# The opening of a two-layer transformer kernel: two head groups' queries first, the other queries and values after the first scores

## The chip, the cores and the metric

The kernel runs on one core of a Trainium2 chip. A core has five engines with instruction queues of their own: TensorE (PE, matrix products; its weight loads are listed as PEld), VectorE (DVE), ScalarE (ACT), GpSimd (POOL) and SyncE (SP, which here issues all DMAs). Each queue is worked off in its order, and queues wait for each other by semaphores. The metric is the device time of one execution in microseconds (us), as the median of several runs.

## The reference, cut to what matters

The input is 2048 tokens of 512 numbers in bf16. Attention and a feed-forward part follow each other twice, with the same weights in both rounds; each works on a layer norm and adds to its input.

```python
def _A_ref(x, wqkv, wo):
    B, S, D = x.shape
    H = 32; Dh = D // H
    qkv = (x @ wqkv).reshape(B, S, 3, H, Dh).transpose(2, 0, 3, 1, 4)
    q, k, v = qkv[0], qkv[1], qkv[2]
    p = _softmax(jnp.einsum("bhqd,bhkd->bhqk", q, k) * Dh ** -0.5, axis=-1)
    o = jnp.einsum("bhqk,bhkd->bhqd", p, v)
    return o.transpose(0, 2, 1, 3).reshape(B, S, D) @ wo

def _B_ref(x, w1, b1, w2, b2):
    y = _layernorm(x, axis=-1)
    h = _gelu(jnp.einsum("bsd,df->bsf", y, w1) + b1)
    return jnp.einsum("bsf,fd->bsd", h, w2) + b2

x = A_x
x = x + _A_ref(_layernorm(x, axis=-1), A_wqkv, A_wo)
x = x + _B_ref(_layernorm(x, axis=-1), B_w1, B_b1, B_w2, B_b2)
x = x + _A_ref(_layernorm(x, axis=-1), A_wqkv, A_wo)
x = x + _B_ref(_layernorm(x, axis=-1), B_w1, B_b1, B_w2, B_b2)
```

There are 32 heads of 16 numbers; four heads form a head group, so there are eight head groups. The work that counts is 32 x 2048 x 2048 exponentials in each of the two attention parts.

## The kernel before, in words

**How the order of the work comes about.** The program is a generator. Jobs (`job_lnqkv`, `job_first_tile`, `flow_scores` and others) are Python coroutines that hand tasks to a planner, `Sched`. A task names its engine, a priority (smaller goes first), its instructions, what they read and write, and for each a written-down duration. The planner plays time forward with these durations: at each step it takes, on the engine that can start first, the ready task of the smallest priority, and appends it to that engine's queue. A changed duration, priority or task can thus change the order of everything after it. Buffers and PSUM banks are handed out by pools (`get` and `release`), and a job can wait for marks set by others (`keys`). A second pass, `refill`, puts products with a zero matrix (`zw`, lines L1307 to L1311) into planned gaps of PE, to keep its clock up.

**Attention.** Tokens are cut into 16 tiles of 128, queries into chunks of 512 (four tiles). A segment is one head group and one chunk of queries over some key tiles; a score tile is one key tile against 512 queries of one head. The first chunk is run in two parts: part 0 takes only the key tiles 0 to 3 for all eight head groups (16 score tiles for each), so that scores can begin when four token tiles have been worked up; part 1 takes the other twelve. `flow_scores` sends score tiles in groups, two tiles alternating between two pairs of banks in part 0, and three and two tiles from part 1 on. ACT takes the exponential of a group (L1386). From part 1 on VectorE takes a share of the tiles with an integer trick (L1478, L1509). PE multiplies the exponentials by the values (L1579). A group of scores needs the scaled queries of its segment (`qt`) and the key and value of its key tile (`kv`).

**The softmax bound.** Each query row carries, as a 17th number in a 32-wide slot, an upper bound of its scores taken from the query's norm and the largest key norm, so that no maximum over scores is needed. For this the keys' squares are summed (`norms`, L992, into `n2k`), the maximum over tokens is taken, its square root formed on POOL (L1109), and two small matmuls spread it (`job_scl`, L1104 to L1113). The queries' side is `bound_rows` (L999 to L1007): an inverse square root by an integer start value and one Newton step, in six small operations.

**The opening.** Three loads of x and three of the weights go out first (`build_startup`). Six buffers for query and key rows (`qk`) have their padding cleared (L724, L725, L758, L759). For each of the first four token tiles `ln_group` makes the norm's statistics on VectorE (L850, L851) and the inverse root on POOL (L858, L859), and `job_first_tile` does the rest: it applies the norm (L870), transposes on PE (L1020) and copies on ACT (L1021), and starts three strands. `keys` multiplies (L1043), copies to bf16 (L1054), squares on ACT (L1057), sums, and stores a transposed copy into KT by DMA (L1047). `queries` multiplies for all 32 heads, copies and squares on ACT (L1066, L1067), sums, forms the bound, transposes the first head group's queries on PE (L1072) and stores all of them to memory (`q_scr`, L1075). `values` multiplies and copies on ACT (L1082). `job_qt` multiplies the queries by the scale (L1144): the first head group straight from PSUM, the others from a transposed load of `q_scr` (L1130). When the queries of all four tiles are on their way to memory (mark `qst`), the tiles 4 to 15 begin: statistics, norm on POOL (L868), a transposing DMA (L904), keys and values (`job_qkv_tile`, L927 to L950), and last their queries. When the keys of all 16 tiles are known, `job_scl` runs again for part 1.

Of the kernel before, what the change touches and what calls it, by code (L numbers as in the profile page):

```python
# [8 lines left out]
BF16 = mybir.dt.bfloat16  # L9
F16 = mybir.dt.float16  # L10
F32 = mybir.dt.float32
I32 = mybir.dt.int32
# [499 lines left out]
class Builder:  # L512
# [45 lines left out]
    def alloc(self, es):  # L558
# [51 lines left out]
        self.qt2 = t("qt2", [128, 4, 32], F32)  # L610
        self.kmx = t("kmx", [32, 4], F32)
# [5 lines left out]
        self.nmr = t("nmr", [128, 16], F32)  # L617
        self.ioi = self.dp[:, 6, 0:256].bitcast(F32)
# [17 lines left out]
        pl["qk"] = Pool(range(3))  # L636
# [49 lines left out]
    def build_startup(self):  # L686
# [28 lines left out]
        dve = lambda fn, reads, writes, dur=0.2: Task("dve", 1.9, [I(fn, reads, writes, dur)])  # L715
# [6 lines left out]
        def pads(eng, b):  # L722
            qv = self.qks(b)
            n0(eng, I(lambda e: e.memset(qv.rearrange("p k (h c) -> p (k h) c", c=32)[:, :, 16:32], 0.0), [], [("qk", b, 0), ("qk", b, 1)], 0.9))  # L724
            n0(eng, I(lambda e: e.memset(qv[:, 1, :].rearrange("p (h c) -> p h c", c=32)[:, :, 16:17], 1.0), [], [("qk", b, 0), ("qk", b, 1)], 0.2))  # L725
# [3 lines left out]
        pads("pool", 0)  # L729
        pads("pool", 1)  # L730
        pads("dve", 2)

        def consts():
            vv = self.V[:, :, :, :, :].rearrange("p g k h d -> p (g k h) d")
            yield dve(lambda e: e.memset(vv[:, :, 16:17], 1.0), [], [("V", hg, kb) for hg in range(8) for kb in range(16)], 0.7)
# [14 lines left out]
    def build_startup_late(self):  # L750
# [4 lines left out]
        def fills():  # L755
            for b in range(3, 6):
                qv = self.qks(b)
                yield Task("pool", 4.0, [I(lambda e, qv=qv: e.memset(qv.rearrange("p k (h c) -> p (k h) c", c=32)[:, :, 16:32], 0.0), [], [("qk", b, 0), ("qk", b, 1)], 0.9),  # L758
                                         I(lambda e, qv=qv: e.memset(qv[:, 1, :].rearrange("p (h c) -> p h c", c=32)[:, :, 16:17], 1.0), [], [("qk", b, 0), ("qk", b, 1)], 0.2)])  # L759
                S_.release("qk", b)  # L760
# [84 lines left out]
    def ln_group(self, tiles, slot, prio, eps1, eps0, shift):  # L845

        for i, tt in enumerate(tiles):
            c = 4 * slot + i
            s = yield ("get", "st")
            yield Task("dve", prio, [I(lambda e, s=s, tt=tt: e.bn_stats(out=self.st[:, s, :], in_=self.xres[:, tt, :]), [("x", tt)], [("st", s)], 0.65)])  # L850
            yield Task("dve", prio, [I(lambda e, s=s, c=c: e.bn_aggr(out=self.mv[:, c, :], in_=self.st[:, s, :]), [("st", s)], [("mv", c)], 0.172)])  # L851
            self.S_.release("st", s)
# [5 lines left out]
        yield Task("pool", prio, [I(lambda e: e.tensor_scalar(out=rs, in0=var, scalar1=eps1, scalar2=eps0, op0=ALU.mult, op1=ALU.add), [("mv", c0 + i) for i in range(n)], [R], 0.2)])  # L858
        yield Task("pool", prio, [I(lambda e: e.tensor_tensor(out=rs, in0=rs, in1=self.cneg[:, 0:n], op=ALU.pow), [R, ("cneg",)], [R], 0.45 + 0.15 * n)])  # L859
# [16 lines left out]
    def job_lnqkv(self, L, tiles, prio, later=None):  # L876
# [6 lines left out]
        for i, tt in enumerate(tiles):  # L883
            if L == 1 and tt < 4:
                self.S_.spawn(self.job_first_tile(tt, slot, i, left, prio), prio)
                continue
# [6 lines left out]
    def job_qkv_tile(self, L, tt, slot, i, left, prio, what):  # L893
# [4 lines left out]
        yield self.ln_apply(tt, slot, i, xnr, RX, prio, "dve" if tt >= 12 else "pool")  # L898
# [87 lines left out]
    def norms(self, dst, res, ss, which):  # L986
# [3 lines left out]
        def fn(e):  # L990
            with self.nc.allow_low_precision(reason="rounded once, in a bound with a margin"):
                return e.tensor_reduce(out=dst, in_=self.sqs(ss)[:, a:a + 32, :], axis=AX.X, op=ALU.add)  # L992
        return I(fn, [("sq", ss, which)], [res], 0.67)

    def bound_rows(self, qs, ns, RN, prio, eng="pool"):

        pads = lambda ap: ap.rearrange("p (h c) -> p h c", c=32)
        QQ = ("qk", qs, 0)
        yield Task("dve", prio, [I(lambda e: e.tensor_scalar(out=self.qy[:, ns, :], in0=self.n2[:, ns, :].bitcast(I32), scalar1=-0.5, scalar2=RSQRT_MAGIC, op0=ALU.mult, op1=ALU.add), RN, [("qy", ns)], 0.18)])  # L999
        y = self.qy[:, ns, :].bitcast(F32)  # L1000
        a, c, x = self.qt1[:, ns, :], self.qt2[:, ns, :], self.n2[:, ns, :]
        RA, RC = ("qt1", ns), ("qt2", ns)
        yield Task(eng, prio, [I(lambda e: e.tensor_tensor(out=a, in0=x, in1=y, op=ALU.mult), RN + [("qy", ns)], [RA], 0.25 if eng == "pool" else 0.2)])
        yield Task(eng, prio, [I(lambda e: e.tensor_tensor(out=c, in0=a, in1=y, op=ALU.mult), [RA, ("qy", ns)], [RC], 0.25 if eng == "pool" else 0.2)])
        yield Task(eng, prio, [I(lambda e: e.tensor_scalar(out=c, in0=c, scalar1=-0.5, scalar2=1.5, op0=ALU.mult, op1=ALU.add), [RC], [RC], 0.217 if eng == "pool" else 0.2)])
        yield Task(eng, prio, [I(lambda e: e.tensor_tensor(out=a, in0=a, in1=c, op=ALU.mult), [RA, RC], [RA], 0.25 if eng == "pool" else 0.2)])
        yield Task(eng, prio, [I(lambda e: e.tensor_scalar(out=pads(self.qks(qs)[:, 0, :])[:, :, 16:17], in0=a.rearrange("p (n o) -> p n o", o=1), scalar1=-MARG, scalar2=0.0, op0=ALU.mult, op1=ALU.add),  # L1007
# [931 lines left out]
```

## Time and profile before

The time is 1595.41 us, the median of three runs (1594.99 to 1596.77). The profiled execution has a span of 1594.1 us.

| what | from the profile |
|---|---|
| busy share of the span | PE 97%, ACT 96%, DVE 91%, POOL 21% |
| exponentials on ACT (L1386) | 1274 instructions, 1449.7 us |
| first exponential starts | 24.77 us |
| first group of three score tiles | 89.60 us |
| DVE busy in the first 24.77 us | 20.04 us |
| ACT busy in the first 24.77 us | 11.73 us |
| POOL busy in the first 24.77 us | 15.07 us |
| matmuls for queries, keys and values of tiles 0 to 3 (L1043) | 10.16 to 21.44 us |
| first matmul for tiles 4 to 15 (L927) | 35.86 us |
| second scale ready to be read (L1113 starts) | 84.56 us |

How to read the profile: a row of the timeline gives the start and the length in us, the engine, the line of the kernel, the operation, what it writes and reads, how many instructions are merged in the row, and in brackets how long the engine stood idle before it and what ended that. In the table of groups the two numbers behind the bar are busy time in us and the mean of one instruction in ns. The chain of waits is followed back from the end: at each step to what released it. A busy PE includes the zero products, and several row-tiled matmuls at once count once.

### The profile page before, as it was taken

To read this page: it belongs to the slowest core of one execution; us is meant where nothing else is said; L and a number is where in the kernel's file an instruction comes from. 1 tells how busy PE (TensorE), PEld (TensorE's weight loads), DVE (VectorE), ACT (ScalarE), POOL (GpSimd) and SP (SyncE) were. 2 spreads that over 40 slices of the span, in tenths; PEclk is the share of its full clock that TensorE was granted. 3 is DMA by queue.
4 is the path that set the end of the run, shared out by engine and by line. 5 is a ranking of instruction groups with operands and counts; after the bars stand their busy time and mean duration, and the time that the engine had idled before them with its cause. 6 is when DMAs were issued, how large, how long until landed. Compare 5 with 4: busy or idle time off the path is not lost.

```text
span 1594.1 us, 39159 instructions
## 1 busy us (share of the span) xinstructions
PE 1538.6 (97%) x16364; PEld 479.4 (30%) x16497; DVE 1450.3 (91%) x3202; ACT 1528.0 (96%) x1357; POOL 333.9 (21%) x574
## 2 busy tenths in 40 slices
PE   9999999999999999999999999999999999999998
PEld 3222222222222222222222223222222222344444
DVE  7689999989999899989999898999899989999793
ACT  6999999999999999989999998999999999999996
POOL 5585312001220012103212217310001000020010
PEclk9999999999999999999999999999999999999999
DMA  6662012112321223223722233211101100221100
GB/s 172 116 142 87 29 31 40 48 41 59 81 48 50 44 53 78 57 53 86 139 44 62 53 68 78 61 25 21 34 14 38 28 19 22 40 48 30 41 25 21
DMA packets 212465, 88.80 MB, mean 56 GB/s; under 512 B 183835, under 2 KB 206656, under 8 KB 212288
## 3 DMA queue, kind: packets, MB, share of 16 engines
q1 hardware_dynamic: 212288, 86.29, 24.0%
q8 instruction: 129, 2.11, 0.6%
q14 instruction: 48, 0.39, 0.1%
HBM read 34.65 MB, written 19.48 MB: 34 GB/s over the span
## 4 chain that ended last, share of the span: by engine, by line
PE 51%; DVE 28%; ACT 17%; issue 2%; POOL 0%; DMA 0%; POOLq 0%; DVEq 0%
PE ps L1401 18%; ACT PT L1386 15%; PE ps L1579 15%; DVE dp L1478 12%; DVE dp L1509 9%; PE ps L1713 4%; PE ps L1756 4%; PE ps L927 3%; PE ps L1307 3%; ACT h L1748 1%; PE ps L1311 1%; PE ps L1658 1%; DVE accT L1609 1%; DVE st L850 1%; DVE n L992 1%
## 5 line engine op out<-in xcount | busy, mean ns | idle before, releaser
L1386 ACT ACTIVATE PT<-ps 128x1536 bf16<-128x1536 f32 (+1 forms) x1274 | 1449.7, 1259 | 38.8 <-PE ps L1401 32.2
L1401 PE MATMUL ps<-QT,KT 32*128 32x512 bf16 (+1 forms) x4608 | 672.3, 358 | 16.8 <-DVE dp L1478 5.5
L1478 DVE TENSOR_SCALAR dp<-ps 128x512 uint16<-128x512 f32 x944 | 632.6, 681 | 61.2 <-PE ps L1401 58.2
L1509 DVE TENSOR_SCALAR dp<-dp 128x1024 uint16<-128x1024 uint16 (+1 forms) x1434 | 557.4, 430 | 7.9 <-PE ps L1579 3.2
L1579 PE MATMUL ps<-PT,V 128*17 128x512 bf16 (+1 forms) x3544 | 467.1, 358 | 0.0
L1579 PE MATMUL ps<-dp,vs 128*17 128x512 bf16 (+1 forms) x3192 | 444.4, 357 | 0.5 <-DVE dp L1509 0.2
L1401 PEld LDWEIGHTS ps<-QT,KT 32*128 32x128 bf16 x4608 | 172.2, 91 | 546.4 <-ACT PT L1386 237.3
L1144 POOL TENSOR_SCALAR QT<-qraw,scl,qbias 128x512 bf16<-128x512 bf16 (+1 forms) x84 | 72.2, 860 | 790.0 <-PE ps L1401 784.8
L1579 PE MATMUL ps<-dp,V 128*17 128x512 bf16 (+1 forms) x1064 | 215.3, 357 | 1.3 <-DVE accT L1609 1.0
L1309 PE MATMUL ps<-zw 32*128 32x444 bf16 (+5 forms) x702 | 193.5, 323 | 0.0
L1579 PEld LDWEIGHTS ps<-dp,vs 128*17 128x17 bf16 x3192 | 111.0, 88 | 130.3 <-issue 106.8
L1579 PEld LDWEIGHTS ps<-PT,V 128*17 128x17 bf16 x3544 | 113.2, 88 | 102.5 <-issue 89.6
L1311 PE MATMUL ps<-zw 128*32 128x448 bf16 (+22 forms) x1477 | 136.5, 323 | 0.4 <-DVE dp L1478 0.2
L1307 PE MATMUL ps<-zw 128*128 128x448 bf16 (+17 forms) x481 | 114.1, 333 | 4.0 <-DVE ps L727 1.7
L1713 PE MATMUL ps<-yT,wf 128*128 128x512 bf16 (+3 forms) x353 | 92.9, 356 | 8.6 <-issue 4.4
L927 PE MATMUL ps<-wqkv,xnT 128*128 128x512 bf16 x299 | 85.8, 382 | 7.6 <-issue 3.5
L1609 DVE STREAM_TRANSPOSE accT<-ps 128x512 f32<-128x512 f32 (+1 forms) x88 | 57.9, 658 | 10.8 <-PE ps L1579 9.9
L1737 DVE TENSOR_SCALAR h<-ps,b1c 128x512 bf16<-128x512 f32 (+2 forms) x88 | 62.3, 708 | 5.0 <-PE ps L1713 4.7
L1579 PEld LDWEIGHTS ps<-dp,V 128*17 128x17 bf16 x1064 | 53.1, 88 | 45.2 <-issue 27.3
L1169 POOL TENSOR_SCALAR vs<-V 128x340 bf16<-128x340 bf16 (+2 forms) x72 | 60.5, 842 | 26.3 <-PE ps L1579 21.2
L1307 PEld LDWEIGHTS ps<-zw 128*128 128x128 bf16 x481 | 37.4, 98 | 74.2 <-issue 46.4
L1311 PEld LDWEIGHTS ps<-zw 128*32 128x32 bf16 x1477 | 49.1, 95 | 22.1 <-DVE dp L1478 4.1
(179 smaller groups left out, 892.2 us busy)
## 6 DMA issues: line engine op xcount, KB each, us to landing
vs<-vs_scr SPq DMA_DIRECT2D x56, 255.0 KB, 2.8
wf<-in_B_w_dram SPq DMA_DIRECT2D x90, 128.0 KB, 2.6
q_scr<-qk SPq DMA_DIRECT2D x22, 256.0 KB, 2.1
k_scr<-qk SPq DMA_DIRECT2D x12, 256.0 KB, 2.0
out_dram<-xres SPq DMA_DIRECT2D x16, 128.0 KB, 1.7
vs_scr<-vs SPq DMA_DIRECT2D x8, 255.0 KB, 2.9
xres<-in_A_x_dram SPq DMA_DIRECT2D x7, 256.0 KB, 3.3
v_scr<-vst SPq DMA_DIRECT2D x12, 136.0 KB, 1.7
```

The lines of the kernel that those rows point to most:

```text
L927: yield Task("pe", prio, [I(lambda e, c=c: e.matmul(self.ps[:, b, :], lhsT=xnT[:, c, :], rhs=self.wqkv[:, c, which * 512:which * 512 + 512 ...
L1144: yield Task(eng, 0.4, [I(lambda e: e.tensor_scalar(out=self.QT[:, q, 0:W], in0=src, scalar1=self.scl[:, k, hg:hg + 1], scalar2=self.qbias ...
L1307: fn = lambda e: e.matmul(self.ps[:, b, 0:w], lhsT=self.zw[:, 0:128], rhs=self.zw[:, 0:w], start=st, stop=st, skip_group_check=True)
L1309: fn = lambda e: e.matmul(self.ps[:, b, 0:w], lhsT=self.zw[32 * p:32 * p + 32, 0:128], rhs=self.zw[32 * p:32 * p + 32, 0:w], start=st, sto ...
L1311: fn = lambda e: e.matmul(self.ps[32 * p:32 * p + 32, b, 0:w], lhsT=self.zw[:, 0:32], rhs=self.zw[:, 0:w], start=st, stop=st, skip_group_c ...
L1386: S_.submit(Task("act", 1e-5 * gi, [I(lambda e, pt=pt, n=n, b0=b0: e.activation(out=self.PT[:, pt:pt + n, :], in_=self.ps[:, b0:b0 + n, :] ...
L1401: return [I(lambda e, kb=kb, i=i: e.matmul(self.ps[:, b, i * W:(i + 1) * W], lhsT=self.KT[32 * hp:32 * hp + 32, hg, kb * 128:(kb + 1) * 12 ...
L1478: self.S_.submit(Task("dve", 0.0, [I(lambda e: e.tensor_scalar(out=self.dp[:, u, w * 512:(w + 1) * 512], in0=self.ps[:, b, :], scalar1=BIT ...
L1509: yield Task("dve", pr, [I(lambda e, k=k, v=v: e.tensor_scalar(out=self.dp[:, v, 0:N], in0=self.dp[:, u, 0:N], scalar1=float(SHIFT[k]), sc ...
L1579: ops.append((nth[j, sh] + 0.1 * i, I(lambda e, hp=hp, v=v, ap=ap[:, i * W:(i + 1) * W], first=first and i == 0, W=W: e.matmul(self.ps[32 ...
L1609: yield Task("dve", 0.3, [I(lambda e: e.transpose(self.accT[:, a, 0:W], self.ps[:, ACCB, 0:W]), [("ps", ACCB)], [RA], 0.17 + 0.535 * W / 5 ...
L1713: yield Task("pe", pr, [I(lambda e, c=c: e.matmul(self.ps[0:M, b, off:off + W], lhsT=self.w1(fc, c), rhs=self.yT[:, c, 0:W], start=(c == 0 ...
```

## The change

Its aim is to put less in front of the first scores. In words:

- Only the queries of the head groups 0 and 1 (128 of 512 columns) are made on the way to the first scores, for all four tiles into one bank (`job_q0`): one copy, one square, one sum and one bound on VectorE for all four tiles together, eight transposes into one bank, and both head groups scaled straight from PSUM.
- The queries of the other six head groups are multiplied after all keys, and their sums and bounds wait until the second head group's queries are scaled (`("qt", 1)`). The store to `q_scr` is in two pieces.
- The value of tile 0 waits for the other queries' matmuls, the values of tiles 1 to 3 for `("qt", 1)`; those of tiles 2 and 3 are copied by VectorE.
- GpSimd has fewer fills: two padding buffers go to ACT and two to VectorE, two and the ones of V remain on GpSimd, and the other fills wait for the fourth tile's key norms. The root's two steps are one task, and tiles 2 and 3 share one norm group. For tiles 4 to 7 the norm is applied by VectorE.
- The query scaling of the first segment of part 1 (index 8) moves from GpSimd to VectorE, and several priorities and written-down durations change.

```diff
         def pads(eng, b):
             qv = self.qks(b)
-            n0(eng, I(lambda e: e.memset(qv.rearrange("p k (h c) -> p (k h) c", c=32)[:, :, 16:32], 0.0), [], [("qk", b, 0), ("qk", b, 1)], 0.9))
...
+            hole = qv.rearrange("p k (h c) -> p (k h) c", c=32)[:, :, 16:32]
+            if eng == "pool":
+                n0("pool", I(lambda e: e.memset(hole, 0.0), [], [("qk", b, 0), ("qk", b, 1)], 0.95))
+            elif eng == "act":
+                n0("act", I(lambda e: e.activation(out=hole, in_=self.zw[:, 0:16].unsqueeze(1).broadcast_to([128, 64, 16]), func=ACTF.Copy), [("zw",)], [("qk", b, 0), ("qk", b, 1)], 1.05))
...
+            n0("dve" if eng == "act" else eng, I(lambda e: e.memset(qv[:, 1, :].rearrange("p (h c) -> p h c", c=32)[:, :, 16:17], 1.0), [], [("qk", b, 0), ("qk", b, 1)], 0.2))
...
-        pads("pool", 0)
-        pads("pool", 1)
-        pads("dve", 2)
+        self.P.free["act"] = 2.0
+        for b in (2, 3):
+            pads("act", b)
+        for b in (0, 1):
+            pads("dve", b)
...
+        for b in (4, 5):
+            pads("pool", b)
...
         def queries():
+            b = self.qfbank
+            yield from mm(0, 128, b, prio - 0.4, 128 * tt)
+            S_.mark(("q0mm", tt))
+            yield ("keys", [("kmm", k) for k in range(4)])
             b = yield ("get", "mb")
-            yield from mm(0, b, prio)
...
+            yield from mm(128, 512, b, prio + 0.4)
+            S_.mark(("qrm", tt))
...
+            yield ("keys", [("qt", 1)])
+            yield Task("dve", prio + 0.2, [self.norms(self.n2[:, ns, 8:32], ("n2", ns), ss, 0, 8)])
+            yield from self.bound_rows(qs, ns, [("n2", ns)], prio - 0.3, "pool", 8)
             done()
...
         def values():
+            yield ("keys", [("qrm", k) for k in range(4)] if tt < 1 else [("qt", 1)])
             b = yield ("get", "mb")
...
+    def job_q0(self):
...
+        S_.submit(Task("act", 0.4, [I(lambda e: e.activation(out=rows[:, :, 0:16], in_=src, func=ACTF.Copy, scale=0.25 * YU), [("ps", b)], Q0, 0.63)]), cb=lambda: S_.release("mb", b))
+        yield Task("act", 0.3, [I(lambda e: e.activation(out=self.q0sq, in_=src, func=ACTF.Square, scale=0.25 * YU), [("ps", b)], [("dp", 6, 1)], 0.63)])
+        yield Task("dve", 0.3, [I(lambda e: e.tensor_reduce(out=self.q0n[:, 0, :], in_=self.q0sq, axis=AX.X, op=ALU.add), [("dp", 6, 1)], [("n2", "q0")], 0.68)])
+        yield from self.bound(*[self.q0n[:, k, :] for k in range(4)], "q0", rows[:, :, 16:17], ("dp", 7, 0), [("n2", "q0")], 0.3, "dve")
...
-        eng = "dve" if sg["i"] < 4 else "pool"
+        eng = "dve" if sg["i"] in (0, 1, 2, 3, 8) else "pool"
...
-        for tt in range(4):
-            S_.spawn(self.job_lnqkv(1, [tt], 1.5 + 0.1 * tt), 1.5 + 0.1 * tt)
+        S_.spawn(self.job_q0(), 0.3)
+        for ts in ([0], [1], [2, 3]):
+            S_.spawn(self.job_lnqkv(1, ts, 1.5 + 0.1 * ts[0]), 1.5 + 0.1 * ts[0])
```

## The prediction

> **What bounds the kernel now.** First view, the page: the sums and the costliest group.
>
> ```profile
> PE 1538.6 (97%) x16364; PEld 479.4 (30%) x16497; DVE 1450.3 (91%) x3202; ACT 1528.0 (96%) x1357; POOL 333.9 (21%) x574
> ...
> L1386 ACT ACTIVATE PT<-ps 128x1536 bf16<-128x1536 f32 (+1 forms) x1274 | 1449.7, 1259 | 38.8 <-PE ps L1401 32.2
> ```
>
> ACT's exponentials take 1449.7 of 1594.1 us. The time is therefore the moment of the first exponential, plus a nearly full ACT, plus a tail. The diff rewrites only the opening, so I then read the order of time on ACT:
>
> ```profile
> 24.77 15.91 ACT L1386 ACTIVATE PT<-ps 128x1024 bf16<-128x1024 f32 x17 [2.69 <-PE ps L1401]
> 40.89 3.87 ACT L1386 ACTIVATE PT<-ps 128x1024 bf16<-128x1024 f32 x4 [0.21 <-PE ps L1401]
> ...
> 89.60 6.88 ACT L1386 ACTIVATE PT<-ps 128x1536 bf16<-128x1536 f32 x6 [0.81 <-PE ps L1401]
> ```
>
> The exponentials start at 24.77. The first part (64 groups of two tiles, 0.97 us each) runs to 89.60, where groups of three begin. It holds 62.1 us of work and some 2.7 us of short gaps. Third view, the timeline of the opening, all engines:
>
> ```profile
> 1.32 0.94 POOL L724 MEMSET qk<- 128x1024 bf16 x1
> 1.58 0.77 DVE L728 TENSOR_SCALAR ident<-dp 128x128 bf16<-128x128 f32 x1
> ...
> 4.47 0.68 DVE L850 BATCH_NORM_STATS2 st<-xres 128x6 f32<-128x512 bf16 x1
> ...
> 11.82 0.57 DVE L870 TENSOR_SCALAR dp<-xres,mv,rs 128x512 bf16<-128x512 bf16 x1
> ...
> 17.83 0.68 DVE L1054 CAST h<-ps 128x512 bf16<-128x512 f32 x1
> ...
> 19.86 0.68 DVE L992 TENSOR_REDUCE n2k<-OT 128x32 bf16<-128x512 bf16 x1
> ...
> 20.57 0.37 DVE L1104 TENSOR_REDUCE nm<-n2k 128x32 bf16<-128x128 bf16 x1
> ...
> 23.70 0.54 DVE L1144 TENSOR_SCALAR QT<-ps,scl,qbias 128x512 bf16<-128x512 bf16 x1
> ```
>
> This is the chain before the first score: norm of the fourth token tile (11.82), its keys copied (17.83), their squared norms summed (19.86), then the maximum, a square root on POOL and two small matmuls (20.57 to 23.70), QT, scores. From the maximum to the first exponential it is 4.2 us. Between 11.82 and 17.83 the keys wait for PE, whose row in the chain of waits is L1043 without a break from 13.78 to 19.40: all queries, keys and values of four tiles, 48 matmuls. Last view, busy time by stretch after the first exponential:
>
> ```profile
> 24.77:35.86 11.09, 10.76 (x92) 3.40 (x92) 7.00 (x19) 11.09 (x13) 5.05 (x11) 1.00 0.61 143
> 35.86:81.50 45.64, 45.06 (x292) 12.65 (x300) 31.22 (x58) 42.80 (x46) 26.43 (x41) 1.00 0.67 114
> 81.50:89.60 8.10, 7.95 (x62) 2.28 (x62) 5.63 (x14) 7.08 (x9) 6.26 (x9) 1.00 0.45 97
> ```
>
> Columns after the length: PE, PEld, DVE, ACT, POOL, granted clock, DMA. From 35.86 to 81.50 PE is full, because keys and values of tiles 4 to 15 (25.42 us of L927) run among the scores. Before 35.86 PE has room: 4.20 of its 10.76 us are zero matmuls (L1307). The second scale (L1113, at 84.56) is needed for the groups of three and stands 5.0 us ahead of them.
>
> **What the Trainium skill says.** "SBUF — State Buffer", section "Who interferes with whom": a tensor_scalar of VectorE in a two-port mode and a GpSimd operation take one port pair in turns, and the later one blocks. The trace agrees: the identity ends at 2.35, just after POOL's memset (2.26), and the four L870 take 585 ns on average where the undisturbed one takes 410. "ScalarE: Activation LUTs", section "What ACT_TABLE_LOAD costs": an ACTIVATE with immediate scale costs 186 ns + 0.833 ns per element. At 512 elements that is 0.61 us, and the V copies (L1082) measure 607 ns, so I use it below. "TensorE: Matmul & The Clock Gate", section "Back-to-back issue gap", gives 81 ns for a 128-column matmul with its load and 131 ns for 512 columns. Here the first is 56 to 60 ns (four transposes in 0.22 to 0.24 us), the second 216 ns (26 in 5.61 us); the trace decides.
>
> **The change part by part.**
>
> Padding fills. Two of six buffers go to ACT, two to VectorE, two stay on POOL, with V's ones. A fill on ACT is 1024 elements, by the page's price 1.04 us; from the table load's end (1.99) they finish near 3.0 and 4.0. This adds a wait: VectorE sets the ones of those two buffers right after, in its fixed order, so it stands until 4.0; its own two fills follow (0.48 + 0.20 wait + 0.09 each, 1.5 us). The first statistics, all norms behind them, then start at 5.6 instead of 4.47: a loss of 1.1 us. If VectorE slips by less, none; both ends are in the range.
>
> Norms. On POOL the square root of tile 0 began at 6.58, 0.9 us after its variance was scaled, because tile 1 stood between; now the two are one task. Tiles 2 and 3 share one root (596 ns each before; for two I take 0.75). POOL no longer runs the fill (L758, L759) that held it from 7.61 to 9.01 and pushed the roots of tiles 2 and 3 to 9.64. I get norms applied at 8.0, 8.8, 10.5 and 10.9, against 7.40, about 8.4, 10.23 and 11.82. So the last tile gains 0.9, the first loses 0.6; the earlier start is eaten by the fills.
>
> PE. Before the last keys now stand 16 key matmuls (3.5 us) and 16 narrow query matmuls (16 × 0.06 to 0.08, 1.0 to 1.3 us). The 16 rest queries come only after all keys, the values after those; before, up to 32 wide ones (6.9 us) were mixed in. Transposes and copies of the last tile put its activations at 12.5; its keys end at 14.2 instead of 17.8. That is the gain proper: 3.6 us.
>
> VectorE to the first score. Last keys copied 14.9; square on ACT 15.6, or 16.2 if it finds the two query activations (0.6 each) ahead; its sum 16.3 to 16.9. The query bound, one reduction (0.68) and six small steps (0.2 each), 1.9 us, now lies at the same place on VectorE; it replaces four reductions and most POOL steps. I count 0.6 to 1.3 of it as delay: sum of the fourth keys at 17.0 to 18.2. Adding 4.2 gives the first exponential at 21.2 to 22.4. I take **21.8**, a gain of 3.0 us.
>
> After the first exponential. V of tile 1 is copied by ACT between early groups: 0.61 us that no longer lies ahead of it. V of tiles 2 and 3 goes to VectorE (7.00 of 11.09 busy), their 12 matmuls (2.6 us) into the 4.20 us of zero matmuls: nothing. The rest queries' eight activations (0.51 each, 4.1 us) fit into ACT's wait for the scale chain: nothing. The second head group's query needs no trip through memory, which was hidden (ready at 29.0, needed near 32): nothing.
>
> The gate behind. Rest bounds wait for the second QT, then run on POOL: 4 × 5 steps of 0.25 us, some 5 us; only then do queries go to memory and tiles 4 to 15 start. Their first keys came 11.1 us after the first exponential; now I get 21.8 + 5.4 (bounds) + 3.4 (statistics) + 1.8 (root, shift) + 0.4 (apply, now VectorE) + 2.9 (transposing DMA) = 35.7, the same absolute time as 35.86. The second scale thus stays near 84.5. With it the groups of three can start from about 86; ACT's own sum gives 89.60 - 3.0 + 0.6 = 87.2. ACT still decides, with 1 us to spare. Every later stage has full ACT and VectorE and the same work, so it moves along. Sum: 3.0 - 0.6 = 2.4 us, **1593.0**.
>
> **Rivals.** (1) More of it arrives: the statistics are not held by the fills, the query bound fits into waits, first exponential at 20.0, the later start also fills the gaps before 89.60. 4.8 - 0.6 + up to 1 gives **1590.2**. For it: POOL idle, PE clear; against: VectorE, busy 20.04 of the first 24.77 us, keeps most of its list. (2) The gain is given back at 89.60: tiles 4 to 15 start 2.5 us later than I reckon, the second scale comes at 87, the groups of three begin at 89 or later: **1595.4**. For it: PE has no room between 35.86 and 81.50. (3) Slower: bounds or the third group's query (due 15 us after the first exponential, after a store of 4 us and a transpose of 2.8) come late and ACT stands 2 to 4 us, or the whole order, which is planned anew from changed times, falls worse by that much; ACT's waits on scores after 160 us sum to 23.3 us, the longest 4.4, so a few more are possible: **1599**.
>
> **How the numbers follow.** Forecast 0.45, rival one 0.27, two 0.15, three 0.13. The new order can move any case by 2 us. Faster by over 0.2% is below 1592.2: a third of the forecast and nearly all of rival one, 0.42. Slower is above 1598.6: most of rival three and a little else, 0.12. The rest, 0.46, is within. The range, 1588.5 to 1598.0, leaves about 0.1 out at each end.
>
> **What would show it.** First exponential between 21.2 and 22.4; first statistics near 5.6; last keys of tile 3 copied near 14.9; one ACT copy of V between early exponentials; first L927 near 35.7; second scale near 84.5; first group of three near 87.2, and the same lead at the end. Wrong if the first exponential comes after 24 or before 20, if ACT stands over 1 us ahead of the third head group, or if the lead at 90 us is not the lead at the end.

## The result and the profile after

The changed kernel takes **1611.63 us** (1610.83 to 1614.65), the kernel before, run beside it, 1595.97. The ratio is 1.0102, 95% interval 1.0084 to 1.0119. It is 16 us slower, outside the range given (1588.5 to 1598.0). The profiled execution has a span of 1609.0 us against 1594.1.

First view, the page of the changed kernel (ACT's exponentials are now L1425):

```profile
PE 1569.3 (98%) x16456; PEld 479.1 (30%) x16456; DVE 1468.4 (91%) x3239; ACT 1526.8 (95%) x1356; POOL 324.2 (20%) x563
...
L1425 ACT ACTIVATE PT<-ps 128x1536 bf16<-128x1536 f32 (+1 forms) x1271 | 1447.2, 1259 | 55.3 <-PE ps L1440 47.9
```

ACT has no more to do than before (1526.8 against 1528.0 us). Its exponentials waited 55.3 us instead of 38.8, and 47.9 instead of 32.2 of that was for scores from PE. So the 15 us are waits. The order of time on ACT shows where:

```profile
23.31 0.61 ACT L1101 ACTIVATE V<-ps 128x512 bf16<-128x512 f32 x1 [1.51 <-PE ps L1055]
23.81 3.10 ACT L1425 ACTIVATE PT<-ps 128x1024 bf16<-128x1024 f32 x3
...
89.89 6.96 ACT L1425 ACTIVATE PT<-ps 128x1536 bf16<-128x1536 f32 x6 [1.79 <-PE ps L1440]
...
972.86 10.49 ACT L1425 ACTIVATE PT<-ps 128x1536 bf16<-128x1536 f32 x9 [13.57 <-PE ps L1440]
```

The first exponential comes 1.0 us earlier (23.81 against 24.77), the first group of three 0.3 us later (89.89 against 89.60). Before 972.86 ACT stands for 13.57 us. By then the second layer's scores against its first twelve key tiles are done; those against the last four begin here, and they need the end of the first layer. I call this place the change of layer. At the same place the kernel before has:

```profile
961.75 11.43 ACT L1386 ACTIVATE PT<-ps 128x1024 bf16<-128x1024 f32 x10 [4.36 <-PE ps L1401]
```

The 88 transposes that end a segment (L1609, now L1648) give the lag in between. The changed kernel is 1.1 us ahead at 91 us, 2.0 behind at 149, 2.8 behind at 864, 12.2 behind at 971, and mostly 11 to 17 behind from there on. The wait at the change of layer (13.57 - 4.36 = 9.2 us) is the largest piece.

**Why ACT stands there.** The second layer's scores against its last four key tiles need the fourth scale, and before it the first layer's last feed-forward: its GELU on ACT, then products, norms and keys. In the kernel before, the GELU's last input is written on VectorE at 877.83 (0.74 us), and its table load starts at 880.24:

```profile
877.83 0.74 DVE L1737 TENSOR_SCALAR h<-ps,b1c 96x512 bf16<-96x512 f32 x1
```
```profile
880.24 1.28 ACT L1748 ACT_TABLE_LOAD   x1
```

In the changed kernel the last input is written 8.5 us later, and then the GELU waits another 12.3 us:

```profile
886.32 0.74 DVE L1776 TENSOR_SCALAR h<-ps,b1c 96x512 bf16<-96x512 f32 x1
```
```profile
899.33 1.28 ACT L1787 ACT_TABLE_LOAD   x1
```

No data are missing in these 12.3 us. The planner has a rule (`job_ffn`): if more than half of the current segment has been scored (`GELU_TO = 0.5`) when the input is ready, the GELU waits until the next segment has 0.3 of its tiles scored (`GELU_FROM`). Before, the input came in a segment's first half, and the rule let it through. Now it comes in the second half; e1 and e2 below test this. The fourth scale follows at 971.23 instead of 959.66.

### The profile page after: what moved, and what is told of

It is laid out like the page before. It is cut to its first block, busy times and chain, and to the rows that moved or that the text cites. A ratio compares the mean times of both kernels' runs of the same rounds, so it can differ in the third digit from the quotient of the medians.

```text
span 1609.0 us, 39254 instructions
## 1 busy us (share of the span) xinstructions
PE 1569.3 (98%) x16456; PEld 479.1 (30%) x16456; DVE 1468.4 (91%) x3239; ACT 1526.8 (95%) x1356; POOL 324.2 (20%) x563
## 4 chain that ended last, share of the span: by engine, by line
PE 51%; DVE 23%; ACT 21%; issue 2%; POOL 2%; DMA 0%; SPq 0%; POOLq 0%; DVEq 0%
ACT PT L1425 20%; PE ps L1440 17%; PE ps L1618 14%; DVE dp L1517 9%; DVE dp L1548 7%; PE ps L1795 5%; PE ps L1752 4%; PE ps L937 3%; PE ps L1346 3%; PE ps L1697 1%; PE ps L1350 1%; ACT h L1787 1%; DVE accT L1648 1%; DVE st L860 1%; PE ps L1348 1%
## 5 line engine op out<-in xcount | busy, mean ns | idle before, releaser
L1425 ACT ACTIVATE PT<-ps 128x1536 bf16<-128x1536 f32 (+1 forms) x1271 | 1447.2, 1259 | 55.3 <-PE ps L1440 47.9
L1618 PE MATMUL ps<-PT,V 128*17 128x512 bf16 (+1 forms) x3535 | 472.5, 358 | 0.0
L1348 PE MATMUL ps<-zw 32*128 32x444 bf16 (+1 forms) x717 | 197.6, 324 | 0.0
L1350 PE MATMUL ps<-zw 128*32 128x448 bf16 (+19 forms) x1350 | 127.6, 323 | 1.8 <-DVE V L960 0.8
L1346 PE MATMUL ps<-zw 128*128 128x448 bf16 (+15 forms) x505 | 118.7, 335 | 4.9 <-DVE dp L1517 2.2
L1752 PE MATMUL ps<-yT,wf 128*128 128x512 bf16 (+3 forms) x396 | 103.0, 360 | 0.9 <-DVE yT L1878 0.5
L937 PE MATMUL ps<-wqkv,xnT 128*128 128x512 bf16 x336 | 92.7, 382 | 3.0 <-DVE qk L943 1.3
L1208 POOL TENSOR_SCALAR vs<-V 128x340 bf16<-128x340 bf16 (+2 forms) x72 | 60.8, 845 | 28.8 <-PE ps L1618 18.9
L1648 DVE STREAM_TRANSPOSE accT<-ps 128x512 f32<-128x512 f32 (+1 forms) x88 | 57.8, 657 | 5.4 <-PE ps L1618 5.2
L1348 PEld LDWEIGHTS ps<-zw 32*128 32x128 bf16 x717 | 54.3, 92 | 1.2
```

The lines of the kernel that those rows point to most:

```text
L937: yield Task("pe", prio, [I(lambda e, c=c: e.matmul(self.ps[:, b, :], lhsT=xnT[:, c, :], rhs=self.wqkv[:, c, which * 512:which * 512 + 512 ...
L1346: fn = lambda e: e.matmul(self.ps[:, b, 0:w], lhsT=self.zw[:, 0:128], rhs=self.zw[:, 0:w], start=st, stop=st, skip_group_check=True)
L1348: fn = lambda e: e.matmul(self.ps[:, b, 0:w], lhsT=self.zw[32 * p:32 * p + 32, 0:128], rhs=self.zw[32 * p:32 * p + 32, 0:w], start=st, sto ...
L1350: fn = lambda e: e.matmul(self.ps[32 * p:32 * p + 32, b, 0:w], lhsT=self.zw[:, 0:32], rhs=self.zw[:, 0:w], start=st, stop=st, skip_group_c ...
L1425: S_.submit(Task("act", 1e-5 * gi, [I(lambda e, pt=pt, n=n, b0=b0: e.activation(out=self.PT[:, pt:pt + n, :], in_=self.ps[:, b0:b0 + n, :] ...
L1618: ops.append((nth[j, sh] + 0.1 * i, I(lambda e, hp=hp, v=v, ap=ap[:, i * W:(i + 1) * W], first=first and i == 0, W=W: e.matmul(self.ps[32 ...
```

## The experiments

Ratios are against the kernel before, run beside each. "The wait" is ACT's wait at the change of layer, 4.36 us before the change and 13.57 after it. In the short diffs a first line starting with - stands for what is replaced.

**1. Is it the held GELU?** The changed kernel without the hold for that one chunk, and the kernel before with the hold forced.

```diff
-            late = sg["nt"] - self.left(sg) > GELU_TO * sg["nt"]
+            late = (L, qc) != (1, 3) and sg["nt"] - self.left(sg) > GELU_TO * sg["nt"]   # e1, after
+            late = (L, qc) == (1, 3) or sg["nt"] - self.left(sg) > GELU_TO * sg["nt"]    # e2, before
```

> The changed kernel, with one condition taken out: the GELU of the first layer's last chunk is no longer held back to the next segment when more than half of the current one has been scored. Theory one (this rule alone costs the 9 us by which ACT's wait at the layer change grew from 4.4 to 13.6 us): that wait falls to 4 to 6 us and the time by 7 to 9 us, to 1602 to 1605. Theory two (the last chunk's feed-forward is late by itself, because the opening's postponed work pushes everything behind it): the wait stays above 10 us and the time within 3 us of 1611.6.

> The kernel before, with the GELU of the first layer's last chunk always held back to the next segment. Nothing of the change is in it. Theory one: ACT's wait at the layer change grows from 4.4 to 14 to 17 us and the time by 9 to 12 us, to 1605 to 1608. Theory two: the kernel before has room there, the wait stays under 8 us and the time under 1600.

Measured: e1 1607.77 us, ratio 1.0075 (1.006 to 1.009), the wait 5.51. e2 1607.86 us, 1.0072 (1.0057 to 1.0087), the wait 16.34:

```profile
970.16 12.75 ACT L1386 ACTIVATE PT<-ps 128x1536 bf16<-128x1536 f32 x11 [16.34 <-PE ps L1401]
```

The hold alone makes the kernel before nearly as slow as the changed one, as theory one has it. Releasing it in the changed kernel shortens the wait as expected, but wins 4 us and not the 7 to 9 of theory one. e1 loses elsewhere: its mean granted clock was 0.996 to 0.998, and its trace shows a clock of 0.59 from 770 to 780 us and 4 us more lag behind it.

**2. What holds up the opening?** On top of e1: VectorE's fills put ahead of what waits for ACT (e3), and fewer zero products in PE's first gap (e4).

```diff
+        n0("dve", ... self.ident ...)      # e3: identity ahead of the ACCB memset; pads("dve") ahead of pads("act")
         n0("dve", ... self.ps[:, ACCB, :] ...)
-        n0("dve", ... self.ident ...)
+            if k == 0:                     # e4: in refill, first gap
+                end = min(end, 6.0)
```

> As the first run, and VectorE makes the identity before it clears the accumulator bank, and its own two padding fills before the ones that wait for ACT. Theory one (VectorE stood until 4.3 us behind GpSimd's fill of V and then behind ACT's fills, and this delays the norms): first statistics at 4.4 to 4.6 instead of 5.65, first exponential 0.6 to 1.2 us earlier than 23.81, time 0 to 1.2 us below the first run. Theory two (the opening is held by the zero matmuls on TensorE and by VectorE's later list): first exponential within 0.3 us of 23.81.

> As the first run, with the zero matmuls ahead of the first transposes cut by about a third. Theory one (in the changed kernel they run until 10.49 us and hold the first transposes, whose input is there at 9.2): first transposes at 9.2 to 9.4 instead of 10.33, first exponential 0.5 to 1.1 us earlier. Theory two (VectorE's list sets the first exponential): transposes earlier, first exponential within 0.3 us of 23.81.

Measured: e3 1608.32 us, first exponential 25.02; the identity started at 1.17 and still ended at 4.50. VectorE's other fills now stood behind it, and the first statistics came at 6.63 instead of 5.65: the opening is 1.3 us later than in e1, which neither theory had. e4 1606.16 us, the first keys 1.1 us earlier (10.40), the first exponential 23.74 as in e1. So this order on VectorE does not help, and the zero products don't set it. In the opening of the changed kernel VectorE and GpSimd (POOL) show what does:

```profile
1.58 2.94 DVE L737 TENSOR_SCALAR ident<-dp 128x128 bf16<-128x128 f32 x1
...
11.10 1.07 DVE L760 CAST rsel<-iogt 128x4 bf16<-128x4 f32 x1
11.17 1.44 DVE L880 TENSOR_SCALAR dp<-xres,mv,rs 128x512 bf16<-128x512 bf16 x2
...
16.91 0.68 DVE L1068 CAST h<-ps 128x512 bf16<-128x512 f32 x1
```
```profile
1.32 2.26 POOL L744 MEMSET V<- 128x512 bf16 x1
3.19 1.25 POOL L729 MEMSET dp<- 128x1024 bf16 x1
...
11.15 0.51 POOL L776 MEMSET wf<- 128x512 bf16 x1
11.62 0.51 POOL L777 MEMSET g<- 128x512 bf16 x1
```

The identity ends at 4.5 instead of 2.35, with the fills of GpSimd beside it. The ones of V moved there; the description of the change says that they remain on GpSimd, but in the kernel before VectorE sets them (L735, at 4.33). A cast of four columns takes 1.07 us at 11.10 while the "other fills" run on GpSimd. They are meant to wait for the fourth tile's key norms, which come at 19.7; that key only places them in GpSimd's queue, and on the chip they run as soon as the queue gets to them, at 10.59.

**3. GpSimd really kept free, bounds earlier, more zero products**, each on top of e1, and all together. e5 also lets the other bounds go early, which its expectation doesn't name.

```diff
-        n0("pool", ... e.memset(vv[:, :, 16:17], 1.0) ...)       # e5: to consts() on dve; pads("dve") ahead of pads("act")
-            yield ("keys", [("n2k", 1, 3)])
+            yield ("keys", [("scl", 1, 0)])                      # e5: the other fills
-FILL_U = 0.55
+FILL_U = 0.65                                                    # e6
-            yield ("keys", [("qt", 1)])
+            yield ("keys", [("n2k", 1, k) for k in range(4)])    # e7 and e5: the other bounds
-            yield ("keys", [("qraw", 2)])
+            yield ("keys", [("qraw", 4)])                        # e7: later loads of x
```

> The changed kernel with the GELU of the first layer's last chunk not held back, and with GpSimd really kept free in the opening: the ones of V go to VectorE as before the change, VectorE's own padding fills stand ahead of those that wait for ScalarE, and GpSimd's other fills come only after the first scale. Theory one (GpSimd's fills block VectorE's port): identity ends near 2.4 us instead of 4.5, first statistics near 4.5 instead of 5.65, the CASTs and the norm between 10 and 12.5 take under 0.7 us, first exponential between 21.0 and 22.5. Theory two (the chain is bound elsewhere, by the copies on ScalarE or by TensorE): first exponential after 23.2 although the blocks are gone. In both the first group of three stays near 89.6, since the second scale is set by tiles 4 to 15, and the time is that of the version with the GELU alone, 1602 to 1608.

> The changed kernel with the GELU not held back, and zero products put into planned gaps of TensorE up to a busy share of 0.65 instead of 0.55. Theory one (the dips of the granted clock near 775 us cost some 4 us of that version's time): the granted clock is 1.0 in the profiled run and its mean within 0.001 of 1.0 in the timed ones, the time 1601 to 1604. Theory two (the dips don't depend on these products, or the added products themselves delay TensorE): clocks of 0.996 to 0.998 again, or 1606 and more.

> The changed kernel with the GELU not held back; the bounds of the other six head groups' queries wait only for the key norms of the first four tiles, not for the second head group's scaled queries, and the loads of x for later tiles stand behind the next two query loads in SyncE's queue instead of ahead of them. Theory one (the lead is given back by 90 us because tiles 4 to 15 start late and the second scale with them): the second transposed norm of tiles 4 to 15 loads before 36 us instead of 37.7, the second scale is ready before 87.0 instead of 87.9, and the first group of three comes at 88.3 to 89.0 instead of 89.6 to 89.9. Theory two (TensorE between 36 and 82 us sets it, whatever the start): second scale at 87.7 to 88.2 again and no change at 90 us. The time follows with 1601 to 1607.

> All of the three together, on the changed kernel with the GELU not held back: GpSimd free in the opening, the other bounds early, more zero products. Theory one (the loss is the held GELU, the dips of the clock, GpSimd's blocks and the late second scale, and these add): first exponential 21 to 22.5, first group of three at 87.0 to 88.5, hole at the change of layer under 6 us, clock within 0.001 of 1.0, time 1598 to 1602. It still has the changed order after 800 us, so by this theory it does not beat the kernel before by more than 0.2%. Theory two (what is gained in the opening is eaten by full VectorE and TensorE up to 160 us, as in the changed kernel): the lag against the kernel before at 150 us is +1.5 or more again, time 1602 to 1606.

| | us (median) | ratio, interval | first exponential | first group of three |
|---|---|---|---|---|
| e5 | 1604.51 | 1.0060, 1.0039 to 1.0081 | 22.86 | 88.54 |
| e6 | 1602.84 | 1.0047, 1.0034 to 1.0061 | 23.74 | 90.24 |
| e7 | 1604.87 | 1.0050, 1.0034 to 1.0065 | 23.97 | 88.55 |
| e8 | 1601.04 | 1.0032, 1.0020 to 1.0045 | 22.86 | 87.65 |

In e5 the blocks are gone:

```profile
1.58 0.77 DVE L737 TENSOR_SCALAR ident<-dp 128x128 bf16<-128x128 f32 x1
...
6.43 0.48 DVE L748 MEMSET V<- 128x512 bf16 x1 [1.69 <-issue]
...
11.04 0.18 DVE L760 CAST rsel<-iogt 128x4 bf16<-128x4 f32 x1
11.12 0.41 DVE L880 TENSOR_SCALAR dp<-xres,mv,rs 128x512 bf16<-128x512 bf16 x1
...
16.11 0.68 DVE L1068 CAST h<-ps 128x512 bf16<-128x512 f32 x1
```

The first exponential moves by 0.95 us, so with all of e5's edits together the blocks cost about that much. It misses the 21.0 to 22.5 expected, and so does e8's: from 14.3 us on VectorE works without a gap through copies, sums and bounds of all four tiles, up to the scaled queries. In e6 three of four runs have a clock of 1.0, and its record shows none of e1's dip: the lag between 747 and 789 us grows by 0.8 us instead of 4.9. e4's record lacks that dip too, with no more zero products, so e6 does not show that these keep it away. In the five runs of e8, 1599.61 to 1601.14 us go with clocks of 0.999 and 1.0, and 1604.48 with 0.996: about 1 us for each 0.001. e5 and e7 give some 1.2 to 1.5 us, but a run of e4 with 0.945 took only 14 us more than its best, so this is no fixed price. In e7 the second transposing load of norms directly follows the first (both in 2.52 us from 31.13), and the second scale is ready 1.3 us earlier than in the changed kernel:

```profile
86.60 0.23 DVE L1153 TENSOR_SCALAR scl<-ps,onesm 128x8 f32<-128x8 f32 x1 [0.27 <-PE ps L1152]
...
88.55 3.80 ACT L1425 ACTIVATE PT<-ps 128x1536 bf16<-128x1536 f32 x3 [1.79 <-PE ps L1440]
```

The first group of three starts 1.95 us after that scale, and 1.95 us after it in the changed kernel (87.94 and 89.89), in e6 (88.29 and 90.24) and in e8 (85.70 and 87.65). So the scale sets it in these orders. In the kernel before, 5.0 us lie between. The scale of e5 comes at 86.60 as well, so its first group of three moved too, which was not expected. If the gains add (e5: opening and bounds 1.3; e7: bounds and loads 1.3; e8: all three 2.2 us against the changed kernel's 87.94), the opening and the order of the loads give 0.9 each and the bounds 0.4. e8 is 0.2 us ahead of the kernel before at 149 us, so its theory two, a lag of 1.5 or more there, fails.

What was left in e8 (5 us; its best run, with a clock of 1.0, is still 4 us behind) was neither the opening nor the GELU's hold nor the clock; the order itself remained as a theory.

**4. Which edit tips the order?** One line alone (e9), only that line taken back (e10), the line taken back with e8's edits but without e1's (e11), and another single line (e12).

```diff
-        eng = "dve" if sg["i"] < 4 else "pool"
+        eng = "dve" if sg["i"] in (0, 1, 2, 3, 8) else "pool"        # e9, on before; reversed in e10 and e11, on after
-... "dve" if tt >= 12 else "pool")
+... "dve" if tt >= 12 or L == 1 and tt < 8 else "pool")              # e12, on before: norm of tiles 4 to 7
```

> The kernel before with one line of the change alone: the query scaling of segment 8, the first of part 1, on VectorE instead of GpSimd. The opening up to the first group of three is untouched. Theory one (the loss is not in the rewritten opening but in the order after it, and this one small task is enough to tip that order): first exponential 24.8 as before, 1271 exponentials instead of 1274, ACT's wait at the change of layer 13 to 17 us instead of 4.4, time 1606 to 1611, which is slower by as much as the whole change. Theory two (the loss needs the rewritten opening): within 2 us of the kernel before.

> The changed kernel with only that line taken back: segment 8 is scaled by GpSimd as before, everything else of the change stays, the rule for the GELU too. Theory one (order): ACT's wait at the change of layer below 6 us with no change to the rule, 1275 exponentials, first exponential and first group of three as in the changed kernel (23.8 and 89.6 to 89.9), time 1597 to 1603. Theory two (the rewritten opening causes the loss): 1608 or more, the long wait again.

> The changed kernel with that line taken back, GpSimd free in the opening, the other bounds early and more zero products; the rule for the GELU as it was. Theory one: first exponential 21.5 to 21.9, first group of three 87.0 to 87.7, no long wait at the change of layer, clock within 0.001 of 1.0, time 1593 to 1598: the lead of 2 to 2.5 us at 90 us would then at last be seen at the end, unless the order after it loses as much. Theory two (any order other than that of the kernel before loses 4 us or more in the middle, clock or not): 1598 to 1603.

> The kernel before with another single line of the change: the norm of tiles 4 to 7 is applied by VectorE instead of GpSimd. This gives another order again (1273 exponentials). Theory one (the time after the opening is a matter of which order the planner falls into, in steps of several us either way): the first group of three within 1 us of 89.6, and from 160 us on a lag or lead that comes and goes by up to 5 us, time 1593 to 1602. Theory two (only orders that hold the GELU back lose): within 2 us of the kernel before.

| | us (median) | ratio, interval | exponentials | first group of three | the wait |
|---|---|---|---|---|---|
| e9 | 1609.04 | 1.0082, 1.0067 to 1.0098 | 1271 | 89.62 | 16.63 |
| e10 | 1599.70 | 1.0024, 1.0015 to 1.0032 | 1275 | 89.69 | 4.05 |
| e11 | 1597.37 | 1.0010, 1.0003 to 1.0016 | 1275 | 87.46 | 4.05 |
| e12 | 1598.53 | 1.0015, 1.0008 to 1.0022 | 1273 | 90.54 | 7.47 |

This settles the main question. One instruction moved from GpSimd to VectorE, with the old opening untouched, makes the kernel 13 us slower. Its groups of three begin at 89.62 (before 89.60), so it costs nothing where it stands. In e9 the GELU's input is written at 880.75, and the GELU is held until 894.78; the wait grows by 12.3 us, which is nearly all of the loss:

```profile
880.75 0.74 DVE L1737 TENSOR_SCALAR h<-ps,b1c 96x512 bf16<-96x512 f32 x1
```
```profile
894.78 1.28 ACT L1748 ACT_TABLE_LOAD   x1
...
970.68 4.62 ACT L1386 ACTIVATE PT<-ps 128x1536 bf16<-128x1536 f32 x4 [16.63 <-PE ps L1401]
```

The changed kernel without that line (e10) is 12 us faster than with it, with the rule of the GELU as it was:

```profile
962.04 8.23 ACT L1425 ACTIVATE PT<-ps 128x1536 bf16<-128x1536 f32 x7 [4.05 <-PE ps L1440]
```

It stays 3.4 us behind the kernel before, so the line is 12 of the 16 us and not all. The lead itself does not reach the end either: e11 has its first exponential at 23.01 (21.5 to 21.9 expected) and its first group of three 2.1 us ahead of the kernel before, and ends 1.0 us behind it. e12 is 2.2 us slower than the kernel before, with a wait of 7.47 us though its GELU was not held (table load at 882.29): another order again, as its theory one has it, but so near to the 2 us of theory two that it settles little.

**5. The work or the order?** The same instruction of another segment on VectorE: segment 10 in the kernel before (e13). Other orders for the changed opening, all without e1's edit: e14 with those of e5, e6 and e7, segment 9 and `GELU_FROM` 0.2; e15 with e5's fills but not its early bounds, with e6, the loads of x from e7, segment 10 and `GELU_TO` 0.6; e16 with the opening as changed, segment 9 and `GELU_FROM` 0.2.

```diff
-        eng = "dve" if sg["i"] < 4 else "pool"
+        eng = "dve" if sg["i"] in (0, 1, 2, 3, 10) else "pool"       # e13, on before
```

> The kernel before with the query scaling of segment 10 on VectorE, where the run with one line of the change had segment 8: the same instruction, the same size, two segments later. Theory one (only the order counts): the opening is that of the kernel before to within 0.1 us, no wait of over 6 us at the change of layer, time 1589 to 1598, far from the 1609 of segment 8. Theory two (the work put on VectorE in part 1 costs it): 1600 or more.

> The version with GpSimd free in the opening, other bounds early and more zero products, with segment 9 scaled by VectorE, and the GELU held only when 0.2 of a segment has not been scored (0.3 before): another order. Theory one (the lead of 2 us at 90 us can be kept where the order is good): first group of three at 87.0 to 87.7, time 1591 to 1596. Theory two (the lead is paid back by work left over at 90 us in every order): 1596 to 1601.

> The version with GpSimd free in the opening and more zero products, the other bounds waiting for the second head group as in the changed kernel, segment 10 scaled by VectorE and the GELU held from 0.6 of a segment on instead of 0.5: another order again, with the same two theories: one, 1591 to 1596; two, 1596 to 1601.

> The changed kernel with its opening as it is, segment 9 instead of 8 scaled by VectorE, and the GELU held only while less than 0.2 of a segment has been scored. Theory one: first exponential 23.8 and first group of three 89.7 to 89.9 as in the changed kernel, no long wait at the change of layer, time 1593 to 1599, some 13 us or more below the changed kernel with the same opening. Theory two (the opening itself costs): 1603 or more.

| | us (median) | ratio, interval |
|---|---|---|
| e13 | 1591.72 | 0.9972, 0.9962 to 0.9983 |
| e14 | 1596.11 | 1.0002, 0.9994 to 1.0010 |
| e15 | 1593.86 | 0.9986, 0.9980 to 0.9993 |
| e16 | 1598.01 | 1.0014, 1.0006 to 1.0021 |

The instruction concerned, in the kernel before, e9 and e13:

```profile
84.97 1.53 POOL L1144 TENSOR_SCALAR QT<-qraw,scl,qbias 128x512 bf16<-128x512 bf16 x2 [0.93 <-DVE scl L1113]
```
```profile
84.92 0.47 DVE L1144 TENSOR_SCALAR QT<-qraw,scl,qbias 128x512 bf16<-128x512 bf16 x1
```
```profile
93.64 0.70 DVE L1144 TENSOR_SCALAR QT<-qraw,scl,qbias 128x512 bf16<-128x512 bf16 x1
```

The work moved is the same; with segment 8 on VectorE the kernel takes 13 us more, with segment 10 it takes 4.4 us less. What differs is what the planner makes of it: the order, and with it how many exponentials ACT takes (1271 and 1274).

```profile
958.86 10.49 ACT L1386 ACTIVATE PT<-ps 128x1536 bf16<-128x1536 f32 x9 [2.09 <-PE ps L1401]
```

In e13 the wait is 2.09 us. e13 beats both kernels, with the old opening, and so does e15 by a little (0.14% under the kernel before), with the new one. e16 has the changed opening as it is and is 13.6 us below the changed kernel's median, with two edits, segment 9 and `GELU_FROM`. e14, at 1596.11 us, lies on the border of its two theories. Two expectations failed here. The first group of three came at 89.95 in e14 and 92.61 in e16, not at 87.0 to 87.7 and 89.7 to 89.9. That group belongs to segment 8. With segment 9 on VectorE, segment 8 stays on GpSimd, and in e16 its scaling stands there behind three scalings of values (L1208, 87.74 to 91.12):

```profile
91.12 0.78 POOL L1183 TENSOR_SCALAR QT<-qraw,scl,qbias 128x512 bf16<-128x512 bf16 x1
```

In e15 the group came at 92.39, with the second scale at 89.86. That is 2.8 us later than in the kernel before, and yet e15 ends ahead of it. The other failed expectation is e13's first exponential, which came at 25.63 instead of 24.77; the last section shows why.

## Why the prediction was wrong

**The step that failed** is "Every later stage has full ACT and VectorE and the same work, so it moves along." The work is the same, but its order is planned anew, and a rule with a threshold (half of a segment) turned a feed-forward input that came 8.5 us later into a GELU 19 us later. Rival three named this ("the whole order, which is planned anew from changed times, falls worse"), on the right side, and mis-sized it: it took 2 to 4 us from ACT's waits in the trace of before (longest 4.4 us). That trace shows the waits of one order, not those of another; the one here is 13.57 us. The edit that tips it, the scaling of segment 8, was named in the description of the change and had no line in the sum; it is worth 12 to 13 us (e9, e10).

**The first exponential**, 21.8 foretold, came at 23.81. The last keys were to be copied by 14.9; their copy ran from 16.91 to 17.59. The norms of the third and fourth tile were applied at 11.17 and 12.21 (10.5 and 10.9 foretold), and the fourth tile's transposed rows were copied by 13.97 (12.5 foretold):

```profile
12.89 1.09 ACT L1034 ACTIVATE yT<-ps 128x512 bf16<-128x512 bf16 x2 [1.05 <-PE ps L1033]
```

PE then ended the last key products at 16.45 (14.2 foretold). It had no gap from 11.49 on, and the key products of three tiles came after 12.9. That PE began late was not the reason: in e4 its first keys came at 10.40, it stood from 11.53 to 12.35, and the last keys ended at 16.44. So the late norms on VectorE and PE's own list after them are the terms that were too small, by 1.3 and 0.8 us; VectorE's copy came 0.5 us later still. What followed was no slower than foretold: the fourth sum ended 2.1 us after the copy (2.1 to 3.3 reckoned, with the query bound in between), and from the maximum to the first exponential it was 4.1 us (4.2). One reading of the trace of before was wrong as well: the stretch of PE from 13.78 to 19.40 holds 26 of the products for queries, keys and values, not all 48.

That the first statistics start at 5.65 (5.6 foretold) was luck. ACT's fills, for which VectorE was to wait, were done at 4.01; VectorE's identity, blocked by GpSimd's fills, ended only at 4.52. One of these fills is V's ones, 2.26 us. The prediction lets them "stay" on GpSimd, so their move from VectorE is in no term. More of GpSimd's fills block the norms at 10.6 to 12.1, which the sum left out too. Without these blocks (e5) the last keys end on PE at 15.68 and the first exponential comes at 22.86.

**The gate behind.** The first product for tiles 4 to 15 starts at 35.86, as before (35.7 foretold). Two errors cancel here: the first exponential came 2.0 us later than foretold, and from there it took 12.05 us instead of 13.9. "The second scale thus stays near 84.5" does not follow from that. It is ready at 87.94:

```profile
87.94 0.23 DVE L1153 TENSOR_SCALAR scl<-ps,onesm 128x8 f32<-128x8 f32 x1 [0.27 <-PE ps L1152]
```

The second transposing load of norms starts on SyncE at 37.74, behind the loads of x. In the kernel before it starts at 34.00, with the third directly behind it:

```profile
34.00 2.57 SPq L904 DMA_TRANSPOSE xnT<-xn  x2
```
```profile
36.09 1.60 SPq L713 DMA_DIRECT2D xres<-in_A_x_dram  x3
37.74 1.84 SPq L914 DMA_TRANSPOSE xnT<-xn  x1
```

One tile on time says nothing of the twelve. So the lead is gone at the first group of three, by the way of rival two. e7 bears this out: with the loads in another order and the bounds let go earlier, 1.3 us of it come back, 0.9 of that by the loads if the gains add. That e7 and e11 still lose their lead by 166 us (e11 is 2.9 us behind there) fits work that was left over at 90 us: in the changed kernel VectorE is busy 74.24 of the 76 us from 90 to 166, before 72.83. No run tried that apart.

**What held:** no wait of ACT for the third head group's query. The one copy of V on ACT came directly ahead of the first exponential (23.31), not after it.

**What stays open.** Which later choice of the planner turns segment 8's half microsecond into another order was not followed step by step. Neither was the rest of e8: with the line taken back (e11) some 4 of its 5 us go, which makes most of it the order's, with no single place named. The 3.4 us that e10 still loses were not followed either.

## What to carry to other kernels

Where a planner writes the order, an edit early in the kernel is two changes: its own saving, and a new order of all that follows. Here the first was worth 1 to 2 us at the first exponential, and the second anything from 4 us less to 13 us more in the time; so try each edit alone and with a neighbour of no meaning (another segment, another number), before calling a loss or a gain the edit's. Look in the plan for rules with a threshold on the long chains, above all where a phase ends and one chain gates everything. And a lead at an early mark is worth only what is done by then: check the work left over, not the mark.

## What the runs showed of the hardware

The ones of V (512 strided elements) show as 2.26 us on GpSimd. On VectorE they show as 0.48 us, but after 1.69 us of standing that nothing explains, in the kernel before (at 4.33) and in e5 (at 6.43) alike. So moving this fill gives VectorE at most about 2.2 us, and the block by GpSimd's 2.26 us took about that from it again (the identity 2.94 us instead of 0.77). A VectorE instruction that begins ahead of GpSimd's fill is not safe from it either: in e3 the identity began at 1.17 and took 3.33 us, through GpSimd's short iotas (to 1.36) and the fills behind them.

The opening of the kernel before is in five records, and its first exponential comes at 24.77 (before), 24.75 (e9), 25.63 (e12), 25.61 (e2) and 25.63 (e13). The Trainium skill, "TensorE: Matmul & The Clock Gate", section "What's actually happening", says that the window by which the clock is released runs free of the kernel's start, so that the moment of the full clock varies by 0.5 us either way. Here the zero products ahead of the first transposes go from 0.37 us apart to 0.19 at 5.77, 5.75, 6.44, 6.56 and 7.57 us, in the same order of records: the moment does vary, by 1.8 us, which is more than the page gives. The first transposes follow at 8.99, 8.97, 9.28, 9.40 and 9.85, and VectorE's norm of the fourth tile at 11.82, 11.81, 12.11, 12.24 and 12.68. In the first two records it ends by 12.39, ahead of two fills of GpSimd; in the other three it is held until these end at 13.3:

```profile
12.11 1.36 DVE L870 TENSOR_SCALAR dp<-xres,mv,rs 128x512 bf16<-128x512 bf16 x1
```

So 0.3 us on PE became 0.9 us at the first exponential, and the first groups of three come at 90.48 to 90.54 in these three records instead of 89.6. The record of the kernel before that the prediction was read from is one of the two early ones; against the others the changed kernel is 1.8 us ahead at the first exponential and 0.6 us ahead at the first group of three. A gain of under 1 us in this opening is thus no larger than what one record differs from the next.

And the clock of PE can dip in the middle: 0.90 on average from 750 to 800 us in the record of e8, 1.00 in that of e6, with the same share of zero products allowed. It differs from run to run of one kernel (e8: 1.0 in three runs, 0.999 and 0.996 in the others) and from kernel to kernel (e1: 0.996 to 0.998 in all four runs; the kernel before, run beside e9 to e12: 1.0 in all 49). What brings a dip was not found.

```profile
750.00:800.00 50.00, 47.81 (x455) 11.82 (x453) 46.29 (x102) 45.14 (x40) 10.80 (x19) 0.90 0.65 118
```
```profile
750.00:800.00 50.00, 47.78 (x508) 12.94 (x505) 49.93 (x113) 47.72 (x43) 13.92 (x22) 1.00 0.67 130
```
